# RWKV attention and squared-ReLU layer on one core: W2 through SyncE's queue, w to all partitions, one pool of PSUM banks, and a new written order

## The chip, the cores and the metric

The kernel runs on one core of a Trainium2 chip. The metric is the time of one execution on the device in microseconds; the time before is the median of three runs, 173.44 us (173.15 to 173.71).

## What is computed

```python
# attention: r, k, v are [4, 8, 768, 48], w and u are [8, 48]; for each batch and head
for t in range(768):
    y[t]  = r[t] @ (state + outer(u * k[t], v[t]))
    state = w[:, None] * state + outer(k[t], v[t])
# x = y as [3072, 384]; w_in [384, 2048], w_out [2048, 384]
h = maximum(x @ w_in, 0)
out = (h * h) @ w_out          # float32, [3072, 384]
```

## The kernel before

The 768 steps of each batch are cut into six chunks of 128 steps. With four batches that makes 24 units, numbered so that units 0 to 3 are the first chunks of the four batches, 4 to 7 the second ones, and so on. Inside a unit the recurrence is turned into matrix products; from chunk to chunk each batch carries its state in a tile, S0W.

A unit goes through these steps. Each has a short name, and the name is the one that stands in the written order.

- `ld` (line 320): three tiles of 192 KB, r, k and v, of 128 rows of 8 heads by 48 numbers.
- `kh`, `rh` (336, 339): k and r times a decay row, to bf16 in a tile `rk`. The rows come from w: `logw` is its logarithm, `WkS` and `WtS` are exponentials of multiples of it. For units 0 to 3 there are early copies of these two rows in PSUM banks (`Wk`, `Wt`).
- `T`, `Tc` (363, 260): eight matmuls against the identity transpose `rk` into PSUM, and a copy takes it to `rkT`. For most units `XB` (369) does both as one DMA transpose.
- `A` (376) and `Bm` (384): the products of keys and queries, in two banks, and their masking to bf16, one `Bm` per bank.
- `P0`, `P1`, `du`, `dv` (342 to 354): the term with u: r times k, times u, summed over the head, times v. `vb` is v in bf16.
- `Y` (392, 394), `xs` (411): the unit's output in PSUM, and its sum with `dv` in bf16.
- `U` (403), `S0` or `ts` and `S` (418 to 424): the state's update.
- `X`, `xTc` (429, 260) or `xX` (436): the output is transposed by TensorE and copied, or by DMA.

The second layer works on groups of units: the first two groups hold one unit, the other eleven two. `F1` (445) is one bank of hidden values: eight steps of six 256-column matmuls for a group of two, four of twelve 128-column ones for a single unit. `re` (453, 455) is the ReLU, `sq` (460 to 464) the square. `F2` (472) sums a quarter of the 2048 hidden values of a unit: four matmuls of 384 columns; four quarters make the output, which `os` copies from PSUM and `out` (509) stores. The last unit of the order is done in two column pieces (`F2c`, line 486). `Z` is warm-up: matmuls of the identity that nobody reads, 512 columns wide where possible.

W1 is eight tiles. Seven come as fp32 through SyncE's queue (`lW`, line 324) and are cast by ScalarE or GpSimd (`cW`, line 260 or 262); there are four staging tiles for them. The eighth W1 tile (piece 2) and the four W2 tiles come through GpSimd's queue, and DMA converts them to bf16 on the way (`W`, line 333).

Nothing here is scheduled automatically. One string, ORDER, lists all steps in time order, each with its engine (A ScalarE, D VectorE, G GpSimd, P TensorE, S SyncE) and, after a slash, the number of the buffer or bank that its result takes. Each engine runs its own steps strictly in that order; semaphores make a step wait for its inputs and for the last reader of its buffer. So `F1.2.5:P/6` is hidden piece 5 of group 2 on TensorE in buffer 6. Before, the eight banks are split: four for the recurrence, two for F1, two for F2.

Of the kernel before, what the change touches and what calls it, by code (L numbers as in the profile page):

```python
# [17 lines left out]
EARLY = 4  # L18
POOLS = dict(ldr=7, ldk=7, ldv=7, ws=0, wsa=4, rk=7, P0=5, dv=5, vb=8, rkT=7, bank=4, bankH=2, bankO=2, Bm=6, xs=5, xT1=2, xT2=3, xT4=1, hr=6, hq=30, os=4, ts=2)
# [3 lines left out]
P0.0:G/1 rh.1:D T.1:P/0 Z.8.4:P Z.5.5:P kh.0:D Tc.1:A/0 Z.6.4:P T.0:P/1 ld.r.2:S/3 Tc.0:A/1 A.0:P/2/3 vb.1:A/0 P0.3:G/2  # L23
du.1:D/0 dv.1:G ld.v.0:S/1 A.1:P/0/1 Z.8.5:P Z.8.4:P P1.0:D ld.k.2:S/3 kh.3:D du.0:D/1 Bm.0.1:D/0 P0.2:G/3 P1.3:D
Bm.1.1:D/1 rh.2:D/3 kh.2:D lW.0.1:S/0 T.3:P/3 Tc.3:A/2 lW.0.6:S/1 Bm.0.0:D/2 ld.v.2:S/2 WtS:A cW.0.1:A P1.2:G lW.0.7:S/2
T.2:P/1 Z.8.5:P Z.8.4:P Z.6.5:P Bm.1.0:D/3 lW.0.0:S/3 cW.0.7:G ld.v.3:S/3 Tc.2:A/3 du.2:D/2 Y.1:P/3 vb.0:A/1 xs.1:D/0
A.2:P/2/0 cW.0.6:A vb.2:D/2 dv.0:G X.1:P/1 Y.0:P/3 lW.0.5:S/0 xTc.1:A/0 Bm.2.0:D/4 Bm.2.1:D/5 lW.0.4:S/2 dv.2:G
A.3:P/1/2 wc:S Z.4.4:P Bm.3.0:D/3 cW.0.0:A W.0.2:G xs.0:D/1 du.3:D/3 vb.3:G/3 lW.0.3:S/1 U.2:P/0 F1.1.3:P/1 Bm.3.1:D/1
Y.2:P/1 xs.2:D/2 re.1.3:A/0 X.0:P/3 F1.1.0:P/0 xTc.0:A/1 F1.0.0:P/1 dv.3:G Y.3:P/2 xs.3:D/3 X.2:P/1 ld.r.4:S/4 U.0:P/3
re.1.0:A/1 xTc.2:A/0 W.1.0:G F1.0.3:P/0 cW.0.5:G W.1.1:G X.3:P/2 cW.0.4:A xTc.3:A sq.1.0:A0/0 re.0.0:D/2 ld.k.4:S/4  # L30
ld.r.5:S/5 U.3:P/1 F1.0.2:P/1 WLcol:A re.0.3:D/3 ld.k.5:S/5 re.0.2:D/4 F1.1.2:P/0 sq.0.0:A0/1 W.1.2:G W.1.3:G ld.k.7:S/6
re.1.2:D/5 F1.2.1:P/1 ld.v.5:S/4 WkS:A F1.2.4:P/0 cW.0.3:G re.2.1:A/1 F1.2.5:P/1 re.2.4:D/2 U.1:P/2 F1.2.7:P/0
sq.0.2:A0/2 re.2.5:A/4 sq.1.3:D2/3 re.2.7:A/0 sq.2.1:D2/4 sq.2.4:D2/5 F1.0.1:P/1 F1.1.1:P/0 sq.0.3:D2/6 re.0.1:A/1
F1.2.3:P/1 re.1.1:A/2 sq.1.1:A0/7 sq.1.2:D2/8 WLm:G F2.0.0:P/1 S0.0:D re.2.3:D/3 F1.2.2:P/0 F2.1.0:P/0 F1.2.6:P/1 S0.3:D
# [12 lines left out]
F2.4.1:P xTc.6:A/2 ld.r.11:S/4 F2.5.1:P ts.7:D/0 re.3.6:A/4 re.3.7:D/3 xTc.7:A F1.4.4:P/1 P0.8:G/4 kh.11:G/6 F1.4.6:P/0
S.4:D ld.r.12:S/5 ld.k.13:S/5 sq.3.7:A0/20 ts.6:D/1 P1.8:D sq.3.4:A0/21 du.8:D/3 ld.r.13:S/6 sq.3.5:A0/22 S.7:D
re.4.4:A/5 A.9:P/3/2 sq.3.6:A0/23 dv.8:G ld.v.11:S/5 re.4.6:A/1 A.8:P/0/1 P1.9:D Bm.8.1:D/4 F1.4.1:P/1 rh.10:G P0.11:G/0
F2.4.2:P Bm.8.0:D/5 XB.10:S/2 vb.9:A/1 F1.4.2:P/0 re.4.1:A/3 Bm.9.0:D/3 Y.8:P/1 Bm.9.1:D/1 U.8:P/0 du.9:D/4 ld.k.14:S/6  # L50
F1.4.3:P/1 P1.11:G xs.8:D/3 sq.4.1:A0/24 re.4.2:A/0 sq.4.2:A0/25 F1.4.0:P/0 dv.9:G sq.4.4:A0/26 U.9:P/3 re.4.0:A/2
rh.11:D F2.4.3:P re.4.3:A/4 sq.4.0:A0/27 os.4:A/2 Y.9:P/2 F1.4.7:P/0 X.8:P/1 XB.11:S/4 sq.4.3:A0/28 xs.9:D/4 F1.4.5:P/1
xTc.8:A/0 ts.8:D/0 F2.6.0:P/0 ld.k.15:S/1 X.9:P/2 P0.13:D/1 rh.13:G/4 F2.5.2:P re.4.7:D/3 P0.10:D/2 re.4.5:A/0 xTc.9:A
ld.r.15:S/0 S.6:D vb.10:A/3 sq.4.7:A0/29 F2.6.1:P S.8:G F1.5.7:P/0 out.4:S F1.5.5:P/1 re.5.7:A/5 F2.5.3:P du.11:D/0
F1.5.1:P/0 ts.9:D/1 P1.10:G A.11:P/1/0 Bm.11.0:D/0 sq.4.5:A0/1 vb.11:A/0 A.10:P/2/3 re.5.5:A/2 F1.5.0:P/1 kh.13:G
sq.5.5:A0/0 F2.6.2:P Bm.11.1:D/2 re.5.1:A/4 Bm.10.1:D/5 F1.5.4:P/0 os.5:A/2 U.11:P/1 du.10:D/2 re.5.0:A/3 U.10:P/0
# [61 lines left out]
def kernel(  # L118
# [443 lines left out]
```

## Time and profile before

| | us |
|---|---|
| median of three runs | 173.44 |
| span of the profiled execution | 172.5 |
| TensorE matmul busy | 161.6 |
| VectorE busy | 130.3 |
| ScalarE busy | 111.1 |
| GpSimd busy | 80.8 |

The span runs from the first to the last instruction of one profiled execution; the times of the runs are a little longer. PE is TensorE, DVE VectorE, ACT ScalarE, POOL GpSimd, SP SyncE; a `q` behind the name means the engine's instruction queue where it issues DMAs or waits. In the groups of instructions a row ends with the total busy time, the mean length of one in ns, the idle time ahead of them, and who ended most of it. In the chain and the timeline a row begins with its start and its length.

### The profile page before, as it was taken

What the parts mean: (1) busy time and instruction counts of PE and PEld (TensorE: products, weight loads), DVE (VectorE), ACT (ScalarE), POOL (GpSimd) and SP (SyncE); (2) the same over time, 40 slices, a digit from 0 to 9 for tenths busy, and PEclk for the clock granted to TensorE, in tenths of its full rate; (3) what the DMA queues carried; (4) which work ended last, traced back from release to release, by engine and by line L of the source; (5) the groups of instructions that cost most, each with busy time, mean ns of one, the idle gap of its engine ahead of it and who ended that gap; (6) DMA issues with size and microseconds to landing.
All of it is one profiled execution on the core that took longest, in us unless ns stands there. A gap on an engine that the chain in (4) does not pass through costs nothing.

```text
span 172.5 us, 4388 instructions
## 1 busy us (share of the span) xinstructions
PE 161.6 (94%) x1702; PEld 121.2 (70%) x1702; DVE 130.3 (76%) x259; ACT 111.1 (64%) x207; POOL 80.8 (47%) x98
## 2 busy tenths in 40 slices
PE   3976799979999999999999999999999999999992
PEld 1444788745788787787778768777778778777671
DVE  5768977739999896598789889888889894538300
ACT  2358787746379899858649647848858726532430
POOL 5644895108659298966937364047660204000000
PEclk9999999999999999999999999999999999999999
DMA  5999899989999989979999997998988330331022
GB/s 99 223 244 306 227 188 207 195 166 200 204 212 184 202 177 214 241 174 184 204 189 215 177 229 153 180 181 186 154 217 159 85 114 4 87 141 48 23 78 84
DMA packets 105588, 29.13 MB, mean 169 GB/s; under 512 B 98008, under 2 KB 105568, under 8 KB 105568
## 3 DMA queue, kind: packets, MB, share of 16 engines
q1 hardware_dynamic: 103672, 26.95, 72.7%
q0 software_dynamic: 1744, 1.77, 6.1%
q8 instruction: 13, 0.21, 0.5%
q10 hardware_dynamic: 152, 0.14, 0.2%
q14 instruction: 7, 0.06, 0.1%
HBM read 20.46 MB, written 4.72 MB: 146 GB/s over the span
## 4 chain that ended last, share of the span: by engine, by line
PE 76%; DMA 12%; SPq 8%; ACT 1%; POOL 1%; issue 1%; DVE 0%; POOLq 0%
PE bank L472 33%; PE bank L445 31%; DMA ldk<-in_k_dram 8%; SPq L320 6%; DMA wsa<-in_moe_w_in_dram 4%; PE bank L376 3%; PE bank L394 2%; PE bank L392 2%; SPq L324 2%; PE bank L403 2%; PE bank L486 2%; PE bank L429 1%; PE bank L363 1%; ACT W L260 1%; POOL urow L218 0%
## 5 line engine op out<-in xcount | busy, mean ns | idle before, releaser
L445 PE MATMUL bank<-xT,W 128*128 128x256 bf16 (+1 forms) x624 | 74.9, 264 | 0.2
L472 PE MATMUL bank<-W,hq 128*128 128x384 bf16 x368 | 69.3, 326 | 0.0
L453 ACT ACTIVATE hr<-bank 128x512 bf16<-128x512 f32 x75 | 44.4, 596 | 32.6 <-PE bank L445 27.1
L445 PEld LDWEIGHTS <-W 128*128 128x128 bf16 x624 | 55.2, 98 | 10.6 <-DVE hr L455 0.3
L472 PEld LDWEIGHTS <-hq 128*128 128x128 bf16 x368 | 34.8, 98 | 17.6
L460 ACT ACTIVATE hq<-hr 128x512 bf16<-128x512 bf16 x65 | 39.1, 628 | 0.3
L384 DVE TENSOR_TENSOR Bm<-bank,maskJT 128x512 bf16<-128x512 f32 x48 | 31.3, 684 | 7.3 <-PE bank L376 7.2
L346 POOL TENSOR_TENSOR P<-P,ub 128x384 f32<-128x384 f32 x15 | 16.1, 1079 | 13.9 <-DVE P L342 13.6
L455 DVE TENSOR_SCALAR hr<-bank 128x512 bf16<-128x512 f32 x21 | 14.3, 687 | 8.5 <-ACT hq L460 3.8
L342 POOL TENSOR_TENSOR P<-ldr,ldk 128x384 f32<-128x384 f32 x14 | 14.3, 1022 | 9.6 <-DMA ldk<-in_k_dram 6.0
L336 POOL TENSOR_TENSOR rk<-ldk,Wkhat 128x384 bf16<-128x384 f32 x10 | 10.0, 996 | 16.9 <-DMA ldk<-in_k_dram 16.9
L411 DVE TENSOR_TENSOR xs<-bank,dv 128x384 bf16<-128x384 f32 x24 | 13.0, 552 | 5.0 <-POOL dv L354 2.8
L354 POOL TENSOR_TENSOR dv<-ldv,du 128x384 f32<-128x384 f32 x18 | 14.8, 829 | 0.0
L349 DVE TENSOR_REDUCE du<-P 128x8 f32<-128x384 f32 x24 | 13.0, 544 | 0.6 <-POOL P L346 0.4
L260 ACT COPY rkT<-bank 128x1024 bf16<-128x1024 bf16 x7 | 7.1, 1012 | 9.1 <-PE bank L363 9.1
L339 POOL TENSOR_TENSOR rk<-ldr,Wt 128x384 bf16<-128x384 f32 x9 | 9.0, 996 | 7.0 <-DMA ldr<-in_r_dram 7.0
L260 ACT CAST vb<-ldv 128x384 bf16<-128x384 f32 x19 | 9.6, 511 | 4.1 <-DMA ldv<-in_v_dram 4.1
L498 PE MATMUL bank<-identity 128*128 128x512 bf16 x29 | 9.5, 471 | 2.7 <-POOL identity masks.py:199 2.7
L260 ACT COPY os<-bank 128x384 f32<-128x384 f32 (+1 forms) x15 | 7.0, 469 | 6.8 <-PE bank L472 4.5
L262 DVE COPY os<-bank 128x384 f32<-128x384 f32 (+1 forms) x10 | 5.2, 524 | 7.9 <-PE bank L486 4.3
L394 PE MATMUL bank<-vb,Bm 128*128 128x48 bf16 x192 | 11.0, 183 | 0.0
L464 DVE TENSOR_TENSOR hq<-hr 128x512 bf16<-128x512 bf16 x27 | 10.9, 432 | 0.0
(66 smaller groups left out, 166.5 us busy)
## 6 DMA issues: line engine op xcount, KB each, us to landing
ldk<-in_k_dram SPq DMA_DIRECT2D x24, 192.0 KB, 3.6
ldr<-in_r_dram SPq DMA_DIRECT2D x24, 192.0 KB, 3.6
ldv<-in_v_dram SPq DMA_DIRECT2D x24, 192.0 KB, 4.0
out_dram<-os SPq DMA_DIRECT2D x23, 192.0 KB, 2.3
wsa<-in_moe_w_in_dram SPq DMA_DIRECT2D x7, 384.0 KB, 5.6
W<-in_moe_w_out_dram POOLq DMA_DIRECT2D x4, 384.0 KB, 9.9
rkT<-rk SPq DMA_TRANSPOSE x17, 3.5
W<-in_moe_w_in_dram POOLq DMA_DIRECT2D x1, 192.0 KB, 6.3
```

The source lines that it names most:

```text
L260: e.copy(o, a)
L342: e.tensor_mul(P0b[slot[f"P{i}"]], loaded("r", i), loaded("k", i))
L346: e.tensor_mul(t, t, ub)
L349: e.tensor_reduce(dub[slot[f"dv{i}"]], P0b[slot[f"P{i}"]], axis=mybir.AxisListType.X, op=ALU.add)
L354: e.tensor_mul(dvb[slot[f"dv{i}"]], loaded("v", i), t)
L384: e.tensor_mul(Bmb[slot[f"Bm{i}{h}"]], heads(bank(f"bA{i}{h}"), 128), mask_b)
L394: e.matmul(y[:, hc, D * h : D * (h + 1)], m[h][:, hc, :], vb[:, 2 * hc + h, :], start=(c == 0), stop=True, skip_group_check=True,)
L445: e.matmul(hp[:, fi, :], W1[f // 2][:, c, 128 * (f % 2) : 128 * (f % 2 + 1)], xt[:, c, :], start=(c == 0), stop=(c == CCH - 1), skip_group ...
L453: e.activation(hr, hp, AF.Relu)
L455: e.tensor_scalar_max(hr, hp, 0.0)
L460: e.activation(hq, hr, AF.Square)
L472: e.matmul(bank(f"bO{i}", "bO")[:, 0:d_model], hqb[slot[f"hq{g},{f // m}"]][:, at : at + L], W2[q][:, f % 4, :], start=(f == 0), stop=(f = ...
```

## The change

The order is written anew, and the code around it takes more forms (some of them, for paired units, are switched off here: PAIRED and EARLY are 0, SPREAD is False).

- W2 comes as eight fp32 tiles of 384 KB through SyncE's queue, each a block of 256 hidden rows, and is cast on chip: five by ScalarE, two by GpSimd, one by VectorE. W1's piece 2 goes the same way. There are nine staging tiles for both.
- w is loaded by one DMA to all 128 partitions, in place of four rows and a shuffle. The early copies of the decay rows in PSUM are gone.
- The eight PSUM banks are one pool; any step may take any bank.
- F2's quarters may be done in any order: a step names its first hidden block and their number, and the first one done starts the sum.
- The loading tiles are six per input in place of seven.
- The order is planned with VectorE and GpSimd held to be exclusive. It loads r and k of unit 4 before W1, group 2's F1 first, W2's quarters in the order 1, 3, 2, 0, group 9 before group 8, and ends with unit 23 in two pieces in place of unit 22. Its warm-up stands in seven blocks in place of seventeen.

Steps that changed engine (before, after): kh on GpSimd 10, 12; rh on GpSimd 9, 12; P0 on VectorE 10, 12; P1 on VectorE 9, 14; S on GpSimd 6, 9; vb on ScalarE 19, 10; xTc on VectorE 0, 9; re on VectorE 21, 26. The counts of T by TensorE, of XB and of xX are the same.

```diff
-EARLY = 4
-POOLS = dict(ldr=7, ldk=7, ldv=7, ws=0, wsa=4, rk=7, ..., bank=4, bankH=2, bankO=2, ...)
+PAIRED = 0
+EARLY = 0
+SPREAD = False
+POOLS = dict(ldr=6, ldk=6, ldv=6, st=9, rk=7, ...)
...
-w:A Z.8.4:P Z.8.5:P Z.8.4:P Z.8.5:P Z.8.4:P Z.8.5:P ld.k.1:S/0 ld.r.1:S/0 u:S shw:D shu:D tab:A ld.r.3:S/1 logw:A
-Z.6.4:P P0.1:G/0 ld.r.0:S/2 ld.k.0:S/1 Wk:A/0 Wt:A/1 kh.1:D/0 ld.v.1:S/0 rh.3:D/1 ld.k.3:S/2 P1.1:G rh.0:D/2 Z.8.5:P
...
+ld.k.1:S/0 ld.r.1:S/0 P0.1:G/0 w:S tab:A logw:A WtS:A u:S shu:D P1.1:D du.1:D/0 rh.1:D/0 WkS:A kh.1:D/0 Z.97.7:P T.1:P/0
+ld.r.2:S/1 rh.2:D/1 ld.r.3:S/2 ld.k.2:S/1 P0.2:D/1 kh.2:D/1 rh.3:D/2 ld.k.3:S/2 P0.3:D/2 Z.15.7:P T.2:P/1 ld.k.0:S/3 kh.3:D/2
+P1.3:G Tc.1:A/0 A.1:P/2/3 Bm.1.1:D/0 Tc.2:A/1 du.3:D/1 Z.16.0:P A.2:P/4/5 T.3:P/6 Tc.3:A/2 ld.v.1:S/0 P1.2:D du.2:D/2
+vb.1:G/0 Bm.1.0:D/1 ld.r.0:S/3 Z.33.3:P Y.1:P/7 P0.0:G/3 kh.0:D/3 rh.0:D/3 A.3:P/0/1 Bm.2.1:D/2 Bm.3.0:D/3 Bm.3.1:D/4
+ld.v.3:S/1 ld.r.4:S/4 rh.4:G/4 T.0:P/3 Tc.0:A/3 A.0:P/6/2 dv.3:G ld.v.2:S/2 vb.2:A/1 Bm.2.0:D/5 Z.5.1:P Y.2:P/5 dv.2:G wc:S
+U.2:P/0 U.1:P/3 Bm.0.0:D/0 xs.2:D/0 Z.9.4:P X.2:P/1 ld.k.4:S/4 kh.4:G/4 vb.3:A/2 Y.3:P/4 T.4:P/6 WLcol:A Bm.0.1:D/1
+ld.v.0:S/3 vb.0:A/3 dv.1:G xs.3:D/1 Z.6.2:P X.3:P/5 Tc.4:A/4 A.4:P/2/4 WLm:G S0.1:D xs.1:D/2 lW.0.5:S/0 X.1:P/3 xTc.3:D/0
+cW.0.5:G xTc.2:D/0 F1.2.5:P/6 lW.0.4:S/1 cW.0.4:A F1.2.4:P/7 lW.0.6:S/2 cW.0.6:A lW.0.7:S/3 xTc.1:A/0 cW.0.7:A P1.0:G
...
+    w_out_p = moe_w_out.rearrange("(s p j) o -> s p (j o)", p=128, j=2)
...
-    def bank(var, kind="b"):
-        return banks[first[kind] + slot[var]]
+    def bank(var):
+        return banks[slot[var]]
...
         def w(e):
-            e.dma_start(out=quarter_rows(wrow), in_=row4(w))
+            if SPREAD:
+                e.dma_start(out=quarter_rows(wrow), in_=row4(w))
+            else:
+                e.dma_start(out=wb, in_=bass.AP(tensor=w.tensor, offset=w.offset, ap=[[0, 128], [1, H * D]]))
...
         def lW(e, a, s):
-            t = wsb[("wsa", "ws")[a]][slot[f"ws{a}{s}"]]
-            e.dma_start(out=rows2(t, s) if a else t, in_=weights(a, s))
+            t = staged(f"ws{a}{s}")
+            if a == 0:
+                e.dma_start(out=t.rearrange("p (c n) -> p c n", c=CCH), in_=w_in_t[:, :, 256 * s : 256 * (s + 1)])
+            else:
+                e.dma_start(out=t, in_=w_out_p[s])
 
         def cW(e, a, s):
...
+            if a == 0:
+                copy(e, W1[s].rearrange("p c (j m) -> p c j m", j=2), t.rearrange("p (c m j) -> p c j m", c=CCH, j=2))
+            else:
+                copy(e, W2[s // 2][:, 2 * (s % 2) : 2 * (s % 2) + 2, :], t.rearrange("p (j o) -> p j o", j=2))
-
-        def W(e, a, s):
-            e.dma_start(out=rows2(W2[s], s) if a else W1[s], in_=weights(a, s))
...
-        def F2(e, i, q):
+        def F2(e, i, f0, nf):
...
-            for f in range(4 * q, 4 * q + 4):
+            for f in range(f0, f0 + nf):
...
+                summed[i] += 1
...
-                    start=(f == 0), stop=(f == FCH - 1), skip_group_check=True,
+                    start=(summed[i] == 1), stop=(summed[i] == FCH), skip_group_check=True,
```

More of the change, by code (lines that the diff above doesn't have):

```diff
@@ L17 @@
 GROUPS = [1, 1, 2, 2, 2, 2, 2, 2, 2, 2, 2, 2, 2]
[L18 to L19 removed]
+PAIRED = 0
+EARLY = 0
+SPREAD = False
+POOLS = dict(ldr=6, ldk=6, ldv=6, st=9, rk=7, P0=5, dv=5, vb=8, rkT=7, Bm=6, xs=5, hr=6, hq=30, os=4, ts=2, xT1=2, xT2=3)
 ORDER = """
[L21 removed]
@@ L52 @@
[L52 to L56, printed above, removed]
@@ L206 @@
     Wt2 = const.tile([128, H, D], FP32, name="Wt2")
+    WkP = [const.tile([128, H, D], FP32, name=f"WkP_{j}") for j in range(2 if PAIRED else 0)]
+    WtP = [const.tile([128, H, D], FP32, name=f"WtP_{j}") for j in range(2 if PAIRED else 0)]
     WLm = const.tile([128, HP, 2 * D], FP32, name="WLm")
@@ L240 @@
+    nc.gpsimd.memset(maskP if PAIRED else maskJT, 1.0)
+    if PAIRED:
+        for p in rows:
+            above(nc.gpsimd, maskP[p, :], L // 2 + 1)
+    else:
+        above(nc.gpsimd, maskJT, L)
     mask_b = bass.AP(
```

412 lines of the change are left out of this document (256 added, 156 removed).

## Prediction

> **What bounds the kernel now.** I read the chain of work that ended last first, then the same chain in order of time, because its shares alone hide that it has two halves.
>
> ```profile
> span 172.5 us, 4388 instructions
> PE 161.6 (94%) x1702; PEld 121.2 (70%) x1702; DVE 130.3 (76%) x259; ACT 111.1 (64%) x207; POOL 80.8 (47%) x98
> PE 76%; DMA 12%; SPq 8%; ACT 1%; POOL 1%; issue 1%; DVE 0%; POOLq 0%
> ```
>
> ```profile
> 24.58 13.90 DMA ldk<-in_k_dram
> 38.50 0.57 DVE rk L336
> 39.12 0.62 PE bank L363 x8
> ...
> 47.27 0.45 PE bank L363 x8
> 47.72 0.66 PE bank L445 x6
> 48.38 0.65 PE bank L472 x4
> ...
> 49.68 0.55 PE bank L376 x16
> ...
> 56.99 0.17 PE bank L429 x3
> ...
> 169.35 0.37 ACT os L260
> ```
>
> From 39.12 us (step T.5) to 169.33 the chain is TensorE and hardly anything else, every matmul step at its own length: F1 0.66, F2 0.65, T 0.45, X 0.17, A half of 0.55 (16 matmuls are two steps). Those 130.2 us fall only if matmul work moves ahead of that point. Before it the chain waits for DMA: the key tile of unit 5 took 13.9 us. So the time is decided by how much TensorE has done when it becomes continuous, and when that is.
>
> The stretches show why that load was late.
>
> ```profile
> 5.00:10.00 5.00, 5.00 (x33) 2.52 (x31) 4.70 (x11) 2.03 (x3) 3.53 (x4) 1.00 1.11 220
> 15.00:17.50 2.50, 2.17 (x31) 1.31 (x29) 1.98 (x6) 2.50 (x5) 0.00 (x0) 1.00 1.10 341
> 30.00:35.00 5.00, 5.00 (x44) 3.85 (x42) 3.45 (x8) 3.96 (x8) 0.78 (x1) 1.00 1.20 195
> W<-in_moe_w_out_dram POOLq DMA_DIRECT2D x4, 384.0 KB, 9.9
> ```
>
> Columns: length, busy time of PE, PEld, DVE, ACT, POOL, then clock, DMA share, GB/s. DMA is full in all three, yet moves 341 GB/s while W1 goes by SyncE's queue and 195 while GpSimd's queue converts W2 to bf16 on the way. The granted clock is 1.00 throughout.
>
> **The change, part by part.**
>
> *DMA.* W2 leaves GpSimd's queue (four issues) and W1's piece 2 too; SyncE's queue gets nine more 384 KB loads. At 220 GB/s a 192 KB tile takes 0.89 us, at 341 a W1 piece 1.15. No row shows W2 in fp32 by SyncE: below it is a W1 piece's 1.15, above it the 195 GB/s of the W2 stretch, 2.0. I take 1.2, near W1, as it is the same size on the same queue without conversion. From a start at 2.0 us unit 5's key stands behind 17 tiles, w's row (0.6) and six W1 pieces: 2.0 + 18 x 0.89 + 0.6 + 6 x 1.15 = 25.5, landed some 0.8 later at 26.3, against 38.5 now. The DMA stall goes. What is late next is engine work. Behind each of W2's pieces on SyncE's queue stand the tiles of units 4 to 8; that is in the sum, since DMA, and not the issuing, sets the queue's pace.
>
> *w and the start.* w's row now is a 192 KB load third in the queue; it lands near 5.3 and its logarithm starts there instead of at 4.38. It is hidden: VectorE first does the shuffle of u, P1.1 and du.1, to 7.1. If that cover were gone it would cost 0.9.
>
> ```profile
> 1.16 0.74 POOL L218 MEMSET urow<- 128x768 bf16 x1
> 2.70 5.18 PE L498 MATMUL bank<-identity 128*128 128x512 bf16 x13 [2.70 <-POOL identity masks.py:199]
> 4.38 0.52 ACT L289 ACTIVATE logw<-wb 128x384 f32<-128x384 f32 x1 [0.73 <-DVE wb L283]
> 6.82 1.02 DVE L339 TENSOR_TENSOR rk<-ldr,bank 128x384 bf16<-128x384 f32 x2 [0.21 <-DMA ldr<-in_r_dram]
> 32.96 2.18 ACT L460 ACTIVATE hq<-hr 128x512 bf16<-128x512 bf16 x4
> ```
>
> The memsets of wrow and urow no longer stand ahead of the identity, so warm-up starts near 1.55 instead of 2.70. Its first block is 24 wide matmuls: eleven at 0.43 (13 took 5.18, the last two less), thirteen at 0.21, to 9.05. T.1 starts there, against 8.26 now. The last two rows give the pace of independent instructions: two of 0.55 in 1.02, four of 0.63 in 2.18, that is 0.08 to 0.1 less than each one's length.
>
> *VectorE until the first F1.* In the new order F1.2.5 needs xTc.2, and VectorE does all before it. From the timeline and the groups:
>
> ```profile
> 16.28 0.36 PE L394 MATMUL bank<-vb,Bm 128*128 128x48 bf16 x8
> ...
> 19.11 0.83 PE L445 MATMUL bank<-xT,W 128*128 128x128 bf16 x12
> ...
> 23.97 4.02 PE L445 MATMUL bank<-xT,W 128*128 128x128 bf16 x42
> ...
> 35.92 1.46 PE L472 MATMUL bank<-W,hq 128*128 128x384 bf16 x8
> ```
>
> The first row is one Y, the second the first F1; the last two are used further down.
>
> ```profile
> L384 DVE TENSOR_TENSOR Bm<-bank,maskJT 128x512 bf16<-128x512 f32 x48 | 31.3, 684 | 7.3 <-PE bank L376 7.2
> L411 DVE TENSOR_TENSOR xs<-bank,dv 128x384 bf16<-128x384 f32 x24 | 13.0, 552 | 5.0 <-POOL dv L354 2.8
> L349 DVE TENSOR_REDUCE du<-P 128x8 f32<-128x384 f32 x24 | 13.0, 544 | 0.6 <-POOL P L346 0.4
> L260 ACT COPY rkT<-bank 128x1024 bf16<-128x1024 bf16 x7 | 7.1, 1012 | 9.1 <-PE bank L363 9.1
> ```
>
> After du.1 (7.1) come rh.1 to kh.3, eight at 0.47: 10.85. Bm.1.1 waits for T.1 (9.05 + 0.6), its copy (1.0) and A.1 (0.45): 11.15, done 11.8; du.3 12.3. P1.2 reads two SBUF tiles while GpSimd runs P0.0 (12.2 to 13.2): I let it wait, done 13.75; du.2 14.3. Bm.1.0, kh.0, rh.0, Bm.2.1, 3.0, 3.1, 2.0, 0.0, xs.2 and Bm.0.1, seven at 0.60 and three at 0.47, end at 19.95. xs.3 waits for Y.3 (20.2), then S0.1, xs.1, and the two copies xTc, whose VectorE cost no row shows (0.35, between the 0.29 of a 128x128 copy and the 0.55 of a 128x384 one in fp32). **F1.2.5 starts at 22.6**; today the first F1 starts at 19.11. The load of its weights is there by 18. That is the price of the early copies of the decay rows in PSUM being gone and of unit 4 being put first.
>
> *ScalarE until F2.0.12.* W2's casts fall on ScalarE (5), GpSimd (2) and VectorE (1).
>
> ```profile
> L260 ACT CAST W<-wsa 128x768 bf16<-128x768 f32 x4 | 3.6, 890 | 0.8 <-DMA wsa<-in_moe_w_in_dram 0.8
> L262 POOL CAST W<-wsa 128x768 bf16<-128x768 f32 x3 | 2.6, 873 | 3.1 <-DMA wsa<-in_moe_w_in_dram 3.1
> L453 ACT ACTIVATE hr<-bank 128x512 bf16<-128x512 f32 x75 | 44.4, 596 | 32.6 <-PE bank L445 27.1
> L460 ACT ACTIVATE hq<-hr 128x512 bf16<-128x512 bf16 x65 | 39.1, 628 | 0.3
> L333 POOL DMA_DIRECT2D W<-in_moe_w_out_dram x4 | 2.9, 745 | 0.0
> ```
>
> GpSimd gives up the issues (2.9 us for W2's four) for two more casts (1.7), so it gains. ScalarE from the end of Tc.4 (21.85) to the cast of W2's eighth 6: six casts 5.3, eleven relus 6.6, seven squares 4.4, two copies 2.0, xTc.1 0.5, together 18.8, less 26 paces of 0.085 = 16.6, to 38.4; waits for F1.2.3, F1.1.1 and T.6 add 0.9: 39.3. The eighth itself landed by 2.0 + 20 x 0.89 + 0.6 + 8 x 1.15 + 4 x 1.2 + 0.8 = 35.2, so the cast waits for ScalarE, not for DMA. Then F2.0.12 and F2.2.12 (1.3), X.4, U.5 (0.34), F2.3.12 (0.65): **F1.3.7 at 41.6**. VectorE's list from xTc.2 to xs.4, 32 instructions, 18.0 less 2.7, ends at 39.2 with 1.4 of waits: as tight. The one pool of banks adds nothing by itself, but puts waits in here: A.5 waits for S0.0's read of bank 1, and Y.4 for re.2.1 in bank 2, some 0.2 each, counted.
>
> *What is left then.* Up to F1.3.7 the new order has done the same 16 F1 steps as the old up to T.5, and two T, two A, two Y, two X and one F2 more: 0.9 + 0.55 + 0.7 + 0.35 + 0.65 = 3.1. So TensorE ends at 41.6 + 130.2 - 3.1 = 168.7 if the first stage loses nothing. It will. The old kernel, with data there, went from F1.0.2 at 23.97 to F2.0.2 at 35.9 through 11.1 us of steps: 0.8 lost in 12 us. With three engines back to back over 19 us I take 1.3, and 0.5 for further two-tile instructions held by GpSimd (below): bounds 0 and 4. TensorE ends at 170.5.
>
> ```profile
> 167.66 0.29 DVE L262 COPY os<-bank 128x128 f32<-128x128 f32 x1 [4.34 <-PE bank L486]
> out_dram<-os ACTq DMA_DIRECT2D x1, 128.0 KB, 1.7
> out_dram<-os SPq DMA_DIRECT2D x1, 64.0 KB, 1.5
> ```
>
> *The end.* Now 3.15 us follow the last matmul (172.5 - 169.35). The last half stored becomes the 64 KB one: 0.08 less copy, 0.2 less transfer: 2.9. Span 173.4. The three runs' median, 173.44, lies 0.95 above the profiled span, so **174.4 us**.
>
> *The lock.* In the start of the new order VectorE has 22 instructions with two SBUF inputs; the early ones now read the decay rows from SBUF.
>
> ```profile
> L336 DVE TENSOR_TENSOR rk<-ldk,Wkhat x10: 547/556/1350, 33.5 to 128.7; 128x384 bf16<-128x384 f32 x10
> L336 DVE TENSOR_TENSOR rk<-ldk,bank x4: 548/552/555, 5.6 to 14.0; 128x384 bf16<-128x384 f32 x4
> L342 POOL TENSOR_TENSOR P<-ldr,ldk x14: 992/998/1312, 4.9 to 128.3; 128x384 f32<-128x384 f32 x14
> ```
>
> With the rows in SBUF the longest took 1.35 (minimum, median, maximum in ns), with them in PSUM none over 0.555. The median says that the order mostly keeps the two apart. The Trainium skill, "SBUF — State Buffer", section "Who interferes with whom", says that a VectorE instruction with two SBUF inputs and a GpSimd one that reads SBUF exclude each other for a whole instruction. By that rule the trace agrees (1.35 is 0.55 and most of 1.0), and the rule speaks against the change; it is the third rival.
>
> **The rivals.**
>
> *Faster.* The first stage loses nothing, P1.2 meets no lock, and F1.3.7 starts at 41.0: TensorE ends at 168.1, time 172.0. For it: GpSimd is freed of its issues, DMA has 3 us in hand. Against: VectorE and ScalarE both without a gap for 19 us.
>
> *Slower: W2's eighths are no faster than now.* At 2.0 each the queue behind them slips by 8 x 0.8 = 6.4. Unit 7's transposed tiles, at 51.8 by the count, land at 58.2; A.7 stands 12.0 us of steps behind F1.3.7, at 55.4: 2.8 lost, 177.2. It decides from 1.65 us an eighth. This is also the case in which the change doesn't do what it says.
>
> *Slower: the lock bites freely.* 22 instructions, each meeting GpSimd half the time (47% busy) and waiting half of 1.0: 5.5, of which 1.5 is counted: 178.4. It decides once VectorE's waits pass its own slack, which is none. Against: today's order loses little this way.
>
> **How the numbers follow.** Forecast 0.47 (173.3 to 175.8), faster 0.28, slow eighths 0.13, lock 0.12. A measurement of this kernel can tell 0.3% (0.5 us) from no change. Faster than 172.9: 0.27; within 172.9 to 174.0: 0.13, the forecast's lower edge; slower 0.60. The range runs from 171.4 (the first rival with 0.6 of early F1 more) to 178.0; what is left out is most of the lock's case and the faster one's edge. Cases of both signs hold most of the chance; the forecast's own range is the one beside it.
>
> **What would show it.** Right: in the chain no DMA wait for a key tile after 20 us; the first F1 near 22.6; ScalarE without a gap from 22 to 39; F1.3.7 near 43; then TensorE alone, ending near 170.5. W2's stage at 300 GB/s or more. Wrong: a first F1 by 20, or after 24.5; a DMA wait at A.7 or at a cast of W2; VectorE's products of 1 us and more before 20 us; waits of several us past 50, which the sum doesn't hold: it takes the second stage to lose as little as today's.

## The result, and the profile after

The changed kernel takes 184.24 us (median of 4 runs, 181.51 to 185.24); the kernel before took 173.57 on the same chip. The ratio is 1.050, with an interval of 1.040 to 1.060. Medians here and below are over all runs, while ratios leave out the chip's slower state (here 185.24 and 184.83 us), so the two need not agree. The forecast was 174.4 us with a range to 178.0: the sign came out as forecast, the size did not. The median lies 6 us beyond the range, and the two runs that the ratio rests on, 181.51 and 183.64, lie 3.5 and 5.6 beyond it.

The head of the changed kernel's page, and its chain by engine:

```profile
span 181.9 us, 4405 instructions
PE 168.1 (92%) x1718; PEld 123.3 (68%) x1718; DVE 149.9 (82%) x275; ACT 105.6 (58%) x187; POOL 85.4 (47%) x100
PE 51%; DVE 35%; issue 6%; ACT 3%; DMA 2%; POOL 2%; DVEq 0%; POOLq 0%; ACTq 0%
```

Before, the chain was 76% TensorE, 12% DMA and 0% VectorE. Now VectorE holds 35% of it, and the wait for a key tile is gone. VectorE is also busy for 149.9 us in place of 130.3, and the steps that it was given account for the smaller part of that: the first experiment below, which leaves VectorE's list as it is, has 133.9, and the same edit of the kernel before 126.6. The rest is instructions that became longer.

Pieces of the same chain in order of time (start, length, what):

```profile
23.93 2.12 PE bank L558 x24
...
41.26 0.55 DVE dv L413
41.80 0.48 DVE xs L524
42.33 0.34 PE bank L542 x3
...
97.28 0.67 issue
97.95 0.34 DVE xT L279
...
99.23 1.20 DVE Bm L471 x2
100.42 1.30 DVE P L401
101.72 0.90 DVE vb L279
...
103.83 1.97 PE bank L558 x18
```

From 39 us on, the chain of before was TensorE alone. Here it leaves TensorE for VectorE again and again, still at 97 us. Two VectorE pieces carry the cause in their length: a product `P` of 1.30 us, where the other four of its line in the chain have 0.47, 0.48, 0.55 and 0.72, and a cast `vb` of 0.90, where the shortest such cast of the run takes 0.34.

How much TensorE loses shows in one long stretch. The columns are length, busy time of PE, PEld, DVE, ACT and POOL, the granted clock, DMA share and GB/s. First the kernel before, then the changed one:

```profile
43.00:148.00 105.00, 105.00 (x1159) 81.14 (x1158) 90.96 (x173) 75.28 (x146) 57.30 (x61) 1.00 0.85 175
```

```profile
43.00:148.00 105.00, 100.07 (x1043) 74.00 (x1041) 96.76 (x166) 60.77 (x113) 62.36 (x66) 1.00 0.86 171
```

TensorE of before has no idle time in these 105 us. The changed kernel's has 4.9 us, at a clock of 1.00, while VectorE is busy 96.76 of 105.

A busy matmul can still be a waiting one, since the ends of matmuls in the profile are modelled. So I also counted the work: every matmul of the trace at its standard length (384 columns in 0.163 us, from four F2 steps in 0.65, others by their columns, `A` at 0.035, warm-up at nothing), summed up to a time, and subtracted from that time. I call the difference **lost**. All the work is 147.9 us in every kernel here.

| lost (us) by | 43 us | 116 us | 148 us | span |
|---|---|---|---|---|
| before | 19.4 | 20.7 | 21.3 | 172.5 |
| changed | 21.8 | 28.1 | 30.7 | 181.9 |
| changed, GpSimd only writes | 20.8 | 22.2 | 24.5 | 175.4 |
| before, GpSimd only writes | 18.7 | 20.7 | 21.2 | 172.5 |
| before, W2 by SyncE (second attempt) | 25.3 | 29.4 | 30.0 | 181.4 |
| changed, squares on ScalarE | 22.4 | 28.9 | 32.1 | 184.7 |
| changed, squares on ScalarE and GpSimd only writes | 22.4 | 29.6 | 30.8 | 183.0 |

Of the 9.4 us between the spans, 2.4 are lost by 43 us and 7.0 between 43 and 148; 0.4 more follows and the shorter end gives 0.4 back. Most of the loss is steady, not one late load: 0.085 us in each of those 105, where before loses 0.018.

The VectorE groups that read two SBUF tiles, in the changed kernel (busy time, mean ns of one):

```profile
L577 DVE TENSOR_TENSOR hq<-hr 128x512 bf16<-128x512 bf16 x31 | 17.1, 568 | 2.9 <-ACT hr L566 2.5
L398 DVE TENSOR_TENSOR rk<-ldr,Wt 128x384 bf16<-128x384 f32 x12 | 9.0, 758 | 0.0
L537 DVE TENSOR_TENSOR S0W<-ts,WLm 128x384 bf16<-128x384 f32 x7 | 6.2, 893 | 0.1
L471 DVE TENSOR_TENSOR Bm<-bank,maskJT 128x512 bf16<-128x512 f32 x48 | 30.9, 681 | 1.2 <-PE bank L458 1.2
```

Before, `rk<-ldr,Wt` had a mean of 630 and `S0W<-ts,WLm` of 616. The last row is one with an input in PSUM: at 681 ns it stands where it stood (684). Counting VectorE instructions that took over a quarter longer than the shortest of their group gives 8 before and 28 now: 25 products of two SBUF tiles and three casts. How one of them comes about, in the start of the changed kernel:

```profile
14.47 1.38 POOL L398 TENSOR_TENSOR rk<-ldr,Wt 128x384 bf16<-128x384 f32 x1 [0.27 <-DMA ldr<-in_r_dram]
...
14.91 1.35 DVE L398 TENSOR_TENSOR rk<-ldr,Wt 128x384 bf16<-128x384 f32 x1
...
16.32 0.40 PE L428 MATMUL bank<-identity,rk 128*128 128x128 bf16 x4 [0.70 <-DVE rk L398]
```

GpSimd (nominal 1.0) and VectorE (nominal 0.55) both stretch while they overlap, and TensorE waits 0.70 us for the result.

### The profile page after: what moved, and what is told of

Its sections match the earlier page's. It is cut to its first block, busy times and chain, and to the rows that moved or that the text cites. A ratio compares the mean times of both kernels' runs of the same rounds, so it can differ in the third digit from the quotient of the medians.

```text
span 181.9 us, 4405 instructions
## 1 busy us (share of the span) xinstructions
PE 168.1 (92%) x1718; PEld 123.3 (68%) x1718; DVE 149.9 (82%) x275; ACT 105.6 (58%) x187; POOL 85.4 (47%) x100
## 4 chain that ended last, share of the span: by engine, by line
PE 51%; DVE 35%; issue 6%; ACT 3%; DMA 2%; POOL 2%; DVEq 0%; POOLq 0%; ACTq 0%
PE bank L586 23%; PE bank L558 17%; DVE Bm L471 6%; DVE hq L577 4%; DVE rk L392 3%; DVE hr L568 3%; DVE rk L398 3%; DVE du L408 2%; PE bank L458 2%; DVE xs L524 2%; DVE P L401 2%; DMA urow<-in_u_dram 2%; PE bank L495 2%; DVE ts L534 2%; DVE P L405 2%
## 5 line engine op out<-in xcount | busy, mean ns | idle before, releaser
L558 PE MATMUL bank<-xT,W 128*128 128x256 bf16 (+1 forms) x624 | 70.5, 264 | 2.0 <-DVE hr L568 1.2
L566 ACT ACTIVATE hr<-bank 128x512 bf16<-128x512 f32 x70 | 40.6, 596 | 41.0 <-PE bank L558 39.6
L413 POOL TENSOR_TENSOR dv<-ldv,du 128x384 f32<-128x384 f32 x17 | 15.2, 901 | 27.2 <-DVE du L408 18.7
L568 DVE TENSOR_SCALAR hr<-bank 128x512 bf16<-128x512 f32 x26 | 17.5, 683 | 6.5 <-PE bank L558 6.4
L577 DVE TENSOR_TENSOR hq<-hr 128x512 bf16<-128x512 bf16 x31 | 17.1, 568 | 2.9 <-ACT hr L566 2.5
L405 POOL TENSOR_TENSOR P<-P,ub 128x384 f32<-128x384 f32 x10 | 10.8, 1084 | 13.9 <-DVE P L401 13.7
L398 POOL TENSOR_TENSOR rk<-ldr,Wt 128x384 bf16<-128x384 f32 x12 | 13.1, 1090 | 4.1 <-DMA ldr<-in_r_dram 4.1
L612 PE MATMUL bank<-identity 128*128 128x512 bf16 x43 | 12.4, 434 | 1.7 <-POOL identity masks.py:199 1.7
L537 POOL TENSOR_TENSOR S0W<-ts,WLm 128x384 bf16<-128x384 f32 x9 | 9.6, 1071 | 6.2 <-PE bank L516 4.0
L458 PE MATMUL bank<-rkT 48*128 48x128 bf16 x192 | 8.8, 218 | 2.3 <-ACT rkT L277 1.7
L495 PEld LDWEIGHTS <-Bm 128*128 128x128 bf16 x192 | 9.7, 98 | 1.6 <-DVE Bm L471 0.7
```

The lines of the kernel that those rows point to most:

```text
L398: e.tensor_mul(scaled("r", i), loaded("r", i), early("WtQ") if i < EARLY else Wt2)
L495: e.matmul(y[:, hc, D * h : D * (h + 1)], m[h][:, hc, :], vb[:, 2 * hc + h, :], start=(i < B), stop=True, skip_group_check=True,)
L558: e.matmul(hp[:, fi, :], W1[f // 2][:, c, 128 * (f % 2) : 128 * (f % 2 + 1)], xt[:, c, :], start=(c == 0), stop=(c == CCH - 1), skip_group ...
L566: e.activation(hr, hp, AF.Relu)
L568: e.tensor_scalar_max(hr, hp, 0.0)
L577: e.tensor_mul(hq, hr, hr)
```

## The experiments

The leading theory: GpSimd and VectorE exclude each other, VectorE's two-input products stretch throughout the run, and TensorE waits for them. The rivals: W2's new path with its casts; the decay rows in SBUF; the new order itself; the granted clock. In the edits below, lines of the written order are cut to the steps around the change.

**GpSimd only writes.** All of GpSimd's products and casts of the changed kernel read and compute one column and fill the tile with a constant, in about the same time as before; the rest of their result is left out.

```diff
+        def tensor_mul(self, o, a, b):
+            nc.gpsimd.tensor_mul(o[:, 0:1, 0:1], a[:, 0:1, 0:1], b[:, 0:1, 0:1])
...
+                nc.gpsimd.memset(o, 0.05)
+                nc.gpsimd.memset(o, 0.05)
...
```

> The changed kernel, but GpSimd's products and casts (kh, rh, P0, P1, S, dv, vb, cW) compute one column and write a constant to the rest, in about the same time; their results are left out. VectorE's list, the order and all waits stay. Lock theory (VectorE's instructions with two SBUF inputs wait for GpSimd's and so make up 18 us of its 150 us): VectorE busy falls to 130 to 135, none of its two-input products is over 0.6 us, TensorE loses 2 to 3 us instead of 9.3 between 43 and 148 us; time 175 to 178. Length theory (VectorE's list is too long by itself, 132 us without any waiting, the lock only lies in its gaps): TensorE still loses 6 us or more there; time 181 or more.

Measured: 177.95 us, ratio 1.017 (1.010 to 1.023) to the kernel before, against 1.050. GpSimd is still busy 84.4 us. The same groups now:

```profile
L595 DVE TENSOR_TENSOR hq<-hr 128x512 bf16<-128x512 bf16 x31 | 12.6, 418 | 3.2 <-ACT hr L584 2.8
L416 DVE TENSOR_TENSOR rk<-ldr,Wt 128x384 bf16<-128x384 f32 x12 | 6.5, 549 | 0.0
L555 DVE TENSOR_TENSOR S0W<-ts,WLm 128x384 bf16<-128x384 f32 x7 | 3.8, 554 | 0.1
```

The stretch is gone; over all two-input products VectorE saves 14.9 us. The long stretch of TensorE:

```profile
43.00:116.00 73.00, 73.00 (x776) 55.21 (x774) 62.66 (x127) 45.48 (x84) 51.00 (x135) 1.00 1.04 200
```

No idle time up to 116 us, and in that stretch it loses 1.4 us where before loses 1.3 and the changed kernel 6.3. So without the lock the new order and its one pool of eight banks are as good there as the old ones. By the profiles the lock accounts for about 6 of the 9.4 us: 5.2 between 43 and 148 us, where the clock is 1.00 in both, and 1.0 in the start, where this profile kept its clock and the changed kernel's did not. By the runs it is 4 to 6 us: at a mean clock of 1.000 this kernel's three runs average 177.65, and the changed kernel's one run at that clock took 181.51, the next, at 0.991, 183.64. From 43 to 148 us TensorE still loses 3.7 us, where 2 to 3 were expected. What remains against the kernel before is 1.4 us of the start and 1.7 us after 116 us.

**The same in the kernel before**, the control for it.

> Edit: the kernel before, with GpSimd's products and casts cut as in the first experiment (one column is read and computed, the rest of the tile is filled with a constant at about the same duration), so that GpSimd and VectorE no longer wait for each other. Lock theory as it now stands (a stretched product costs only where nothing is left to do for TensorE while it runs; the order of before has that slack): before has 8.0 us of stretch in VectorE's instructions, and nearly nothing comes back: 173.5 to 175.2 us, ratio .992 to 1.002. Rival (every stretched product costs its part, and before pays as the changed kernel does, only less): the changed kernel won about 6 us for 16 us of stretch, so before would win about 2 to 3 us: 171.5 to 172.8.

Measured: 174.80, ratio 1.002 (0.999 to 1.005). VectorE's two-input products give back 3.8 us here, half of the 8.0 that I had put, for instance

```profile
L357 DVE TENSOR_TENSOR rk<-ldr,Wt 128x384 bf16<-128x384 f32 x11 | 6.1, 550 | 0.8 <-DMA ldr<-in_r_dram 0.8
```

against 6.9, and the time doesn't move. A stretched product has no price of its own. The old order gains nothing from 3.8 us less, the new one gains 4 to 6 from 14.9 less. It also shows that constant data alone didn't make this kernel faster.

**W2 by GpSimd's queue** in the changed kernel: four transfers, converted to bf16 on the way, at the places of the first load of each quarter, and no casts.

```diff
-lW.1.2:S/6 cW.1.2:D A.6:P/6/4
+W.1.1:G A.6:P/6/4
...
```

> The changed kernel with W2 in four transfers by GpSimd's queue, converted to bf16 on the way, and without W2's eight casts; W1's eighth piece stays with SyncE. If W2's eighths and their casts are what costs, the time falls by 2 us or more. Lock theory: the end of the start stage stays within 2 us of the changed kernel's (the DMA wait of today's kernel returns, the casts go) and TensorE loses the same 9 us later: 183 to 187.

Measured: 184.19, ratio 1.054 (1.048 to 1.059), the changed kernel's own. Windows of this kernel, then of the changed one, while W2 moves:

```profile
35.00:40.00 5.00, 5.00 (x62) 3.85 (x60) 4.41 (x9) 4.94 (x10) 4.06 (x5) 1.00 0.81 161
40.00:45.00 5.00, 3.70 (x51) 2.58 (x49) 4.20 (x7) 2.13 (x4) 4.03 (x6) 1.00 1.03 155
```

```profile
35.00:40.00 5.00, 4.87 (x54) 3.85 (x54) 5.00 (x10) 4.87 (x9) 3.20 (x4) 1.00 1.05 283
40.00:45.00 5.00, 4.29 (x56) 2.98 (x54) 3.86 (x9) 4.14 (x7) 2.00 (x2) 1.00 1.03 324
```

The path decides nothing: 30.8 us are lost by 148 us here, 30.7 there. Nor do these windows show that SyncE's queue is twice as fast, though their last column (GB/s) reads 161 and 155 against 283 and 324. The profile counts a converting transfer by the bf16 bytes that it writes, and those are half of the fp32 bytes of the same rows. From the pages, first of this kernel, then of the changed one:

```profile
q1 hardware_dynamic: 104216, 27.54, 70.6%
q0 software_dynamic: 1088, 1.57, 5.4%
W<-in_moe_w_out_dram POOLq DMA_DIRECT2D x4, 384.0 KB, 6.3
```

```profile
q1 hardware_dynamic: 105368, 30.69, 76.4%
st<-in_moe_w_out_dram SPq DMA_DIRECT2D x8, 384.0 KB, 5.4
```

W2's 2048 x 384 numbers count as 1.57 MB on GpSimd's queue, two bytes each, and as 3.15 more MB on SyncE's, four bytes each. In the time that its packets took on the 16 DMA engines, W2 has 5.4% of 182.1 us by the first path, 9.8 us, and by the second the 5.8 points that SyncE's queue has more there, some 10 us: no less.

**W2 by SyncE in the kernel before**, with the old order. The first attempt:

```diff
-W.1.0:G F1.0.3:P/0
+lW.1.0:S/4 lW.1.1:S/5 F1.0.3:P/0
...
-W.1.2:G W.1.3:G ld.k.7:S/6
+lW.1.4:S/3 lW.1.5:S/0 lW.1.6:S/1 lW.1.7:S/2 ld.k.7:S/6
...
-F2.0.0:P/1
+cW.1.0:A cW.1.1:G F2.0.0:P/1
...
```

> The kernel before, its order and banks, with W2 as fp32 eighths and W1's piece 2 through SyncE's queue and cast on chip (W2 three by ScalarE, five by GpSimd). This is one part of the change alone. If that part is sound, W2's stage moves at 280 GB/s or more, the wait for unit 5's key goes, and the time falls by 0.5 to 1.5 us: 172 to 173. If the casts or the longer SyncE queue cost more than the transfer saves: 174 to 177.

Measured: 189.24, ratio 1.081 (1.074 to 1.088). This answers nothing: I had listed the load of W2's eighth 6 into a staging tile ahead of the cast of W1's piece 3 from that tile, so W1's piece 3 holds rows of W2, and GpSimd waited for the wrong load:

```profile
37.36 0.86 POOL L262 CAST W<-wsa 128x768 bf16<-128x768 f32 x1 [13.40 <-DMA wsa<-in_moe_w_out_dram]
```

Mended, with that load behind the cast:

```diff
-lW.1.5:S/0 lW.1.6:S/1 lW.1.7:S/2
+lW.1.5:S/0 lW.1.7:S/2
...
-cW.0.3:G re.2.1:A/1
+cW.0.3:G lW.1.6:S/1 re.2.1:A/1
```

> Edit: the kernel before, with its own order and engines, but W2's eighths and the third piece of W1 by SyncE's queue in fp32 and cast on the chip by ScalarE and GpSimd; the load of W2's eighth 6 now stands behind the cast that frees its tile. Theory (this part of the change by itself is sound; the loss is the lock between VectorE and GpSimd): the wait of 13.9 us for a key in the start goes, and the second stage of before stays as it was, so 171 to 175 us, no slower than before. Rival (the casts, twelve more of 0.7 to 1.4 us on two engines in the start, cost more than the wait that goes, whatever the lock does): 176 to 181 us.

Measured: 185.23, ratio 1.057 (1.047 to 1.066). Neither expectation fits: it has the rival's sign, and is 4 us above its range. The key that GpSimd waits for in before is waited for still, and now casts stand behind it on GpSimd:

```profile
39.47 0.99 POOL L340 TENSOR_TENSOR rk<-ldk,Wkhat 128x384 bf16<-128x384 f32 x1 [5.53 <-DMA ldk<-in_k_dram]
40.40 0.82 POOL L262 CAST W<-wsa 128x768 bf16<-128x768 f32 x1
```

TensorE waits 5.1 us for one cast of GpSimd. By 43 us 25.3 us are lost, by 49 us 28.0; from there to 148 us it loses 2.0, and before 1.8. So the casts need an order made for them, which the changed kernel has: its start loses 2.4 us, this one's 5.9. It also separates the two halves once more: the old order's second stage, with W2's new path, stays sound.

**Before without the early rows in PSUM.** The first units read the decay rows from SBUF, which is one part of the change alone.

```diff
-e.tensor_mul(rk[...], loaded("k", i), early("WkP") if i < EARLY else Wkhat)
+e.tensor_mul(rk[...], loaded("k", i), Wkhat)
```

> The kernel before without the early copies of the two decay rows in PSUM; units 0 to 3 read them from SBUF like the others. One part of the change alone. Lock theory: of the eight early products on VectorE those that meet GpSimd's take 1 us and more; the first F1 comes 0.5 to 2 us later, but the DMA wait up to 38.5 us hides most of it: 173.4 to 174.5. Length theory: no difference.

Measured: 175.02, ratio 1.002 (0.998 to 1.005). It is 1.5 us behind at 22 us (17.7 lost, before 16.2), and level at 40 us, where before waits for the key in any case. Its cover is that wait; the changed kernel has none.

**Relief for VectorE.** Two edits of the changed kernel, each taking some 17 us of instructions from VectorE: either all its 31 squares (two SBUF inputs) go to ScalarE, or all its 26 relus (input in PSUM). One line of each:

```diff
-sq.2.2:D2/3
+sq.2.2:A0/3
...
-re.2.7:D/5
+re.2.7:A/5
...
```

> Edit: the changed kernel with all 31 squares that VectorE computes (two SBUF inputs) given to ScalarE; everything else, the order too, as it was. Lock theory (VectorE's two-input products wait out GpSimd's instructions, and TensorE then waits for VectorE): VectorE's busy time falls by about 17 us (31 times 568 ns), less than five stretched instructions fewer for each ten that leave, and most of the steady loss of 7 us between 43 and 148 us goes: 177 to 180 us. Rival (the order: VectorE and ScalarE are late because the new order asks for their results sooner, with or without the lock): ScalarE, at 122 us busy, is late in VectorE's place, 183 to 186 us.

> Edit: the changed kernel with 26 of VectorE's relus (PSUM input, not in the lock) given to ScalarE; the lock's users stay where they are. It takes about 17.5 us of plain work from VectorE, as much as the squares, but no lock user. If the stretch costs because VectorE is full (82% busy, so that a stretched instruction delays the relu that TensorE waits for), slack heals it as well: 177 to 180 us, with the number of stretched products as before (about 29). If a stretched product costs wherever it stands, the time stays at 182 to 184 us.

Measured: 186.44 (ratio 1.069, 1.061 to 1.077) and 192.63 (1.102, 1.095 to 1.110): both slower than the changed kernel. What I expected of the lock failed in both, and the first comes near its rival's 183 to 186. VectorE fell to 134.0 and 136.7 us, ScalarE rose only to 120.7 and 116.8, and neither is full. The waits of TensorE with the squares on ScalarE (us in total, times, longest):

```profile
PE bank L586 <- ACT hq L573: 4.2, 8, 1.8
```

And of VectorE, with the relus there:

```profile
DVE hq L577 <- ACT hr L566: 25.2, 10, 5.9
```

In this fixed list the moved steps land at places where the freer engine is not free. Is this the lock all the same? The squares moved, with the lock gone:

> Edit: the changed kernel with both edits, GpSimd writing only (as in the first experiment, 177.95 us) and all squares on ScalarE (186.44 us with the lock). If moving the squares failed since ScalarE's own order has no room for them (TensorE waits 4.2 us for ScalarE's squares in its profile), that cost shows here too, without any lock: 180 to 183 us. If ScalarE is late only because the lock delays the relus that it waits for, the two gains add or at least don't cancel: 177 to 178.5 us.

Measured: 184.98, ratio 1.057 (1.049 to 1.065), where the lock's removal alone gave 177.95. The move costs 7 us without any lock, 2 more than the most that I had allowed for:

```profile
PE bank L604 <- ACT hq L591: 5.2, 9, 2.0
```

So those two runs say nothing against the lock, and nothing for it. They say that this order has no room on ScalarE at those places, and that an engine's idle share doesn't show room. With the squares on ScalarE the lock's removal also gains little: 186.44 against 184.98 us, with intervals that overlap, though it takes 9.4 us of stretch from VectorE's remaining products. The 4 to 6 us above are what the lock costs in the changed order, not a price that it has in others.

**More warm-up**, against the clock's dip.

```diff
-Z.33.3:P
+Z.40.3:P
...
-Z.5.1:P
+Z.24.1:P
...
-Z.9.4:P
+Z.16.4:P
...
-Z.6.2:P
+Z.16.2:P
```

> Edit: the changed kernel with longer groups of the warm-up matmuls in the start (40, 24, 16 and 16 in place of 33, 5, 9 and 6), which fill TensorE's idle time at 9 to 20 us. If the dip of the granted clock at 15 to 25 us (.82 to .84) is what the start loses against before, the clock stays at 1.0 and the time comes to 181 to 182.5 us; if the start's loss is the late rows of VectorE and GpSimd, nothing changes or the added matmuls delay the first units: 183.5 to 187 us.

Measured: 185.55 (182.53 to 188.60), ratio 1.048 (1.039 to 1.058), against the changed kernel's 1.050. The start in the changed kernel, then with more warm-up (the clock is the third column from the end):

```profile
15.00:20.00 5.00, 3.11 (x43) 2.00 (x41) 4.93 (x8) 2.55 (x6) 4.94 (x7) 0.84 0.95 253
20.00:25.00 5.00, 4.39 (x51) 3.52 (x50) 3.95 (x9) 2.81 (x4) 2.96 (x4) 0.82 1.03 322
```

```profile
15.00:20.00 5.00, 3.90 (x58) 2.53 (x57) 4.12 (x9) 2.55 (x6) 3.86 (x4) 1.00 0.92 195
20.00:25.00 5.00, 4.91 (x56) 3.22 (x53) 4.55 (x10) 2.78 (x4) 4.33 (x7) 1.00 1.00 316
```

The profiled run kept its clock and has the same span, 181.9 us: 18.9 us lost by 25 us in both, and the first F1 at 23.51 in place of 23.76. So keeping the clock this way gains nothing. What the dip costs by itself the run can't say, since the added warm-up also stands in the way: unit 2's output step starts at 19.38 us in place of 18.71.

**The key of unit 5 in the kernel before.** Since DMA was where before waited, two tries to improve it: unit 5's loads ahead of W2's, and W2's second half later.

```diff
-A.3:P/1/2 wc:S Z.4.4:P
+A.3:P/1/2 ld.k.5:S/5 ld.r.5:S/5 wc:S Z.4.4:P
...
-ld.r.5:S/5 U.3:P/1
+U.3:P/1
...
-re.0.3:D/3 ld.k.5:S/5
+re.0.3:D/3
```

```diff
-sq.0.0:A0/1 W.1.2:G W.1.3:G ld.k.7:S/6
+sq.0.0:A0/1 ld.k.7:S/6
...
-cW.0.3:G re.2.1:A/1
+cW.0.3:G W.1.2:G re.2.1:A/1
...
-P0.4:G/4 sq.0.1:D2/9
+P0.4:G/4 W.1.3:G sq.0.1:D2/9
```

> Edit: the kernel before, with SyncE's loads of unit 5's key and receptance issued ahead of the column of w and of W1's piece 3, and so ahead of all of W2's transfers; nothing else. If the wait of 8.6 us of GpSimd for that key, with TensorE's stop of 1.6 us behind it, is a matter of who stands first in the queues, the key is there by 30 us and the time falls by 1 to 2 us: 172.5 to 174 us. If the transfers of that stretch limit it anyway (300 GB/s and more), what is put ahead makes W1's piece 3 or W2 late: 174.5 to 177 us.

> Edit: the kernel before, with the issue of W2's third and fourth quarter on GpSimd moved behind the cast of W1's piece 3 and the first product of unit 4. If W2's first half alone leaves the queues free for unit 5's key, TensorE's stop of 1.6 us at 39 us goes and W2's second half still comes ahead of its first use: 172.5 to 174 us. If the second half is then what TensorE waits for: 175 to 180 us.

Measured: 178.17 (ratio 1.021, 1.015 to 1.026) and 174.46 (0.9995, 0.996 to 1.004). The first is slower than either of its two expectations, the second shows no change. In the first, GpSimd waits for W1 and for another key instead:

```profile
POOL W L262 <- DMA wsa<-in_moe_w_in_dram: 6.6, 2, 3.8
POOL P L342 <- DMA ldk<-in_k_dram: 6.2, 1, 6.2
```

and ScalarE waits 3.64 us for the column of w, with a relu behind it for which TensorE stops 3.37 us. In the second, the wait for the key stays:

```profile
POOL rk L336 <- DMA ldk<-in_k_dram: 9.3, 1, 9.3
```

The 13.9 us of the key in before's chain are worth at most the 1.6 us by which TensorE stops there, and neither try got them. No version here beats the kernel before.

**The stop at 125 us.** Without the lock one stop remains in the second stage; the timeline of that kernel there:

```profile
124.03 0.51 ACT L279 CAST vb<-ldv 128x384 bf16<-128x384 f32 x1 [1.60 <-DMA ldv<-in_v_dram]
124.45 0.59 ACT L584 ACTIVATE hr<-bank 128x512 bf16<-128x512 f32 x1
...
125.09 0.81 PE L576 MATMUL bank<-xT,W 128*128 128x256 bf16 x6 [1.40 <-ACT hr L584]
```

A cast waits for a load of values, a relu stands behind it, and TensorE behind that. The cast moved behind the next two relus, without and with the lock:

```diff
-Bm.21.1:D/0 vb.21:A/5 rh.20:G/5
+Bm.21.1:D/0 rh.20:G/5
...
-re.8.1:A/1 sq.8.1:A0/14
+re.8.1:A/1 sq.8.1:A0/14 vb.21:A/5
```

> Edit: the changed kernel with GpSimd writing only (177.95 us) and, besides, ScalarE's cast of unit 21's values moved behind the two relus and squares that follow it in the list. If the stop of 1.40 us at 125 us comes from that place in the order: 176 to 177 us, ratio about 1.008 to the kernel before. If something behind it is late as well, it stays at 177.5 to 178.5 us.

> Edit: the changed kernel with only ScalarE's cast of unit 21's values moved behind the two relus and squares that follow it. With the lock, TensorE stops there for VectorE (1.21 us, behind two stretched products), and ScalarE's cast has no wait of its own: no difference, 183 to 185.5 us. If the two causes add: 182 to 183 us.

Measured: 178.12 (ratio 1.022, 1.017 to 1.026), no gain, and 185.89 (1.066, 1.063 to 1.070), none either: with a mean clock of 0.98 to 0.99 in all its runs it is rather slower than the changed kernel, for which I have no explanation. Without the lock the stop moved to 127.6 us, where TensorE now waits for a transposed tile:

```profile
PE bank L476 <- DMA rkT<-rk: 1.2, 1, 1.2
```

Both the values and this transpose come by SyncE's queue, so that queue is late there; which of its steps makes it late I didn't find out.

## Why the prediction was wrong, point by point

- **The stall of 13.9 us goes: right.** No wait for a key stands in the chain after 20 us, and while W2 moves the windows show 283 and 324 GB/s, where 300 or more was named. But what W2's path costs was priced from 1.2 to 2.0 us an eighth, as the hinge of a rival, and giving the path back changed nothing (1.054 against 1.050). Nothing hung on it. The reading behind the 2.0 was also wrong: the 195 GB/s count W2 by its bf16 bytes, half of its fp32 bytes, so they were no rate for an fp32 eighth, and the 341 beside it doesn't show that the conversion slows the transfer.
- **Warm-up and T.1: right.** T.1 starts at 8.68 for 9.05 forecast. The shorter end: 2.75 us for 2.9.
- **The first F1 at 22.6: late by 1.2.** It starts at 23.76 (in the chain, which counts from the end of the step before it, at 23.93); without the lock at 22.70, which is within 0.1 of the forecast sum. P1.2, which I let wait for GpSimd, ran in its 0.55; the stretched ones were rh on both engines at 14.5 to 16.3, and VectorE's 1.35 us there was one of the signs named for being wrong. Of the 3.5 us that the sum gave to the early rows in PSUM and unit 4's place together, the rows alone cost 1.5 by 22 us in the kernel before.
- **F1.3.7 at 43.4: late by 1.4**, at 44.79. ScalarE was busy 15.6 of the 17 us from 22 to 39, nearly as forecast. So the sum for the start was sound but for the 1.4 us.

```profile
44.79 1.47 PE L558 MATMUL bank<-xT,W 128*128 128x256 bf16 x12
```

- **Then TensorE alone, ending at 170.5: the step that failed.** It ends at 179.15. I carried the 130.2 us of TensorE's continuous stretch over from before unchanged, less 3.1 for work already done: 127.1 from F1.3.7 on. It took 134.4, which is 7.3 of the 8.5 us between the forecast span and the measured one. "What would show it" names the condition, that the second stage loses as little as today's, and I gave it no price. It lost 8.9 us from 43 to 148 where before lost 1.9.
- **The lock: right mechanism, counted over the wrong stretch.** The rival priced 22 instructions of the start (5.5 us, of which 1.5 was in the forecast) and stopped there. The start lost 2.4 us more than before in all, for whatever reason; the other 7 came after it, and 5.2 of them went with the lock. The reason that I gave against it, "today's order loses little this way", is a statement on the old order. By the counts of the groups, VectorE now has 95 products of two SBUF tiles where it had 83, and GpSimd 87 products and casts for 79. By what the trace of before showed, products of up to 1.35 us with a median of 0.55, the old order mostly kept them apart: 8 of the 83 were stretched. The new one was planned with the two exclusive, and 25 of its 95 were.
- The Trainium skill's rule ("SBUF — State Buffer", section "Who interferes with whom") names only GpSimd instructions that read SBUF, not those that only write it. The runs agree with both halves: 1.35 and 1.38 us while two products overlap, 0.55 once GpSimd only fills tiles. The price comes from the runs alone: 0 us for 3.8 us of stretch in one order, 4 to 6 for 14.9 in the other.

**What stays open.** About 3 us of the difference are not the lock's. 1.4 are lost by 43 us: the first F1 comes at 22.70 even without the lock, against 19.11, and before pays 1.6 of those 3.6 back at its key. 1.7 are lost after 116 us, tied to SyncE's queue near 125 us, and not traced to one step. Whether a few of the stretched products are to blame, rather than their sum, wasn't tried. And as the price by runs goes from 4 to 6 us with the run of the changed kernel that one takes, up to 2 us of it may belong to the clock.

## What to carry to other kernels

When an order is written anew, price the long steady stretch again and not only the part that the change is about: count the instructions that share a resource there, and where an engine is as full as VectorE is here (82%, 76% before), ask which of the stretched ones TensorE waits for. Take the shared resource out of one engine by an edit that keeps its time, in the old order as well as in the new: 3.8 us of stretch were worth nothing in one, 14.9 were worth 4 to 6 in the other. Before comparing the GB/s of two paths, see which bytes are counted. In a list with fixed order, moving work to an engine with idle time is a change of order too, and can cost more than what it relieves.

## What the runs showed of the hardware

- The stretch is mutual: GpSimd's product took 1.38 us for a nominal 1.0 while VectorE's took 1.35 for 0.55.
- VectorE's casts from SBUF to SBUF stretch as well, though they read one tile: of the four casts `vb`, two took 0.98 us and two 0.34 to 0.35; with GpSimd only writing, all four took 0.35.
- By the time of its packets, W2 took the DMA engines as long with the conversion to bf16 on the way, through GpSimd's queue (9.8 us of all 16), as in fp32 through SyncE's (some 10).
- The granted clock fell at 15 to 25 us in the changed kernel, to 0.84 and 0.82, with TensorE busy 3.11 and 4.39 of each 5 us. With more warm-up it stayed at 1.00 (3.90 and 4.91), and in the first attempt with W2 by SyncE it was 0.50 after TensorE had stood for 10.0 us:

```profile
40.00:45.00 5.00, 4.21 (x21) 2.58 (x20) 3.24 (x6) 1.95 (x3) 5.00 (x6) 0.50 1.06 208
```

- An idle TensorE alone doesn't decide it: before's order without the early rows had TensorE busy 3.55 of the 5 us from 10 to 15 and 3.09 from 15 to 20, at 1.00.
- The time does not simply follow the mean clock of the run: the changed kernel took 181.51 us at 1.000 and 183.64 at 0.991, but with W2 by GpSimd's queue it was 184.20 at 1.000 and 183.87 at 0.991.
